# A decode kernel for attention plus gated FFN: TensorE's loop in nine guarded rounds, FFN down projection first, last loads in another order

## The chip, the cores and the metric

One core of one Trainium2 chip runs the kernel. The metric is the device time of one execution in microseconds (us). Executions of one kernel mostly agree within 0.1%. E1 to E7 and E12 below ran on one chip, E8 to E11 on another; the ratios compare each with the kernel before on its own chip.

## The reference, cut to what matters

```
x: 448 values;  16 query heads, 8 key/value heads, 65536 cached positions, head size 256, bf16
g = sigmoid(sum(x * gate_w))
a = attention(x @ wq, k_cache, v_cache) @ wo          # k_cache, v_cache: 268 MB each
b = (relu(x @ W_gate) * (x @ W_up)) @ W_down
out = g * a + (1 - g) * b                             # 448 values
```

Each cached key and value is used once, so 549 MB must come in from memory for very little arithmetic.

## The kernel before

K and V come in tiles of 8.39 MB (128 partitions x 64 KB) into three ring buffers, four K and four V tiles per key/value head, 32 of each (numbered 0 to 31 below). SyncE issues all loads in a fixed order on one queue; a load waits until the tile that had its buffer has been used. VectorE transposes a K tile in eight pieces, TensorE computes scores (64 matmuls), ScalarE exponentiates, TensorE multiplies with V tiles (64 matmuls each).

Which buffer a load takes, and so which earlier tile it waits for, is decided here:

```python
NW = H - 3
for i in range(NT - NTH + 1, NT - 1):
    order.append(("v", i, TILE))                  # V tiles 29, 30
order.append(("wo", 0, 7.3))                      # first part of wo
PIECES = [(0, 64), (64, 96), (96, 112), (112, 120), (120, 128)]
for i, (lo, hi) in enumerate(PIECES):             # V tile 31 in five pieces
    order.append(("vp", i, TILE * (hi - lo) / U))
...
ROUND = (0, 1, 2, 0, 1, 0, 2, 1)
    sl = r if m < 0 else ROUND[m % 8] if m < 8 * (H - 1) else m % 8 % 3
```

At the end this gives: K tile 31 buffer 0, V 28 buffer 1, V 29 buffer 2 (K tile 30's), V 30 buffer 0 (K tile 31's), wo buffer 1, V 31 buffer 2.

TensorE's program is straight code up to the last K tile of head 0, then a loop of seven rounds over a head each, then straight code. Inside the loop TensorE waits for a semaphore `go` that GpSimd raises once per operation (the relay), so that one loop body serves rounds that wait for different values:

```python
def emit_loop(self, its, eng, go):
    with eng.Fori(0, len(its)):
        for o in its[0]:
            eng.wait_ge(go, 1).then_inc(go, -1)
            o.fn(eng).then_inc(self.esem["pe"], 1)
```

The FFN down projection frees buffer 2 for K tile 2, and stands behind all scores of K tile 0: `max(tg + 12.2, tL["wd", 0])` sorts it there.

Of the kernel before, what the change touches and what calls it, by code (L numbers as in the profile page):

```python
# [7 lines left out]
F32 = mybir.dt.float32  # L8
# [16 lines left out]
class _Plan:  # L25
# [8 lines left out]
    def op(self, eng, key, fn, deps=()):  # L34
        o = _Op(eng, key, fn, deps)
        self.ops.append(o)
        return o

    def dma(self, eng, key, sem, fn, deps=()):
        if sem not in self.dsem:  # L40
            self.dsem[sem] = self.es.enter_context(self.nc.semaphore("d_" + sem))
        o = _Op(eng, key, fn, deps, dma=sem)
        self.ops.append(o)
        return o
# [25 lines left out]
                    o.count = ndma[o.dma]  # L70
        return progs

    def relay(self, progs, loops):

        for its in loops:
            for it in its:
                assert [o.fn.__code__ for o in it] == [o.fn.__code__ for o in its[0]]
                for o in it:
                    assert any(d.eng != "pe" for d in o.deps)
                    g = _Op("gp", o.key, None, o.deps)  # L80
                    progs["gp"].append(g)

    def emit_loop(self, its, eng, go):
        with eng.Fori(0, len(its)):
            for o in its[0]:
                eng.wait_ge(go, 1).then_inc(go, -1)  # L86
                o.fn(eng).then_inc(self.esem["pe"], 1)

    def emit(self, e, prog, eng, go=None, seen=None):
        seen = {} if seen is None else seen  # L90
# [19 lines left out]
def bass_gated_mix__gqa_block_cached__glu_gated_reglu__decode_kernel(  # L110
# [13 lines left out]
    H = A_k_cache.shape[1]  # L124
    S = A_k_cache.shape[2]
    DH = A_k_cache.shape[3]
    D = A_x.shape[2]
    F = B_W_gate.shape[1]
    NQ = A_wq.shape[1]
    J = 2 * H  # L130
    U = 128
    TK = 128 * U
    NTH = S // TK
    NT = H * NTH
    R3 = D // 128
# [10 lines left out]
    with es:  # L146
        sb = lambda name, shape, dt: es.enter_context(nc.sbuf_tensor(name, shape, dt))
        ps = lambda name, shape, dt: es.enter_context(nc.psum_tensor(name, shape, dt))

        ring = [sb("ring%d" % i, [128, U * DH], BF) for i in range(NRING)]  # L150
        P_sb = sb("P_sb", [128, 2048], BF)
        ptp = sb("ptp", [128, 1024], BF)
        scr = sb("scr", [128, 1024], BF)
# [20 lines left out]
        hT = sb("hT", [128, FT], BF)  # L174
# [2 lines left out]

        xw = P_sb[:, 0:NX * 160]
        iot = P_sb[:, 800:1056].bitcast(I32)
        qn = P_sb[:, 1056:1312]  # L180
        x_row = P_sb[0:1, 1312:1312 + D]
        fin_o = P_sb[0:1, 0:D]
        gw_row = scr[0:1, 0:D]
        xeo = scr[0:1, 448:704]
        qrep = scr[:, 704:960]
        gtmp = ptp[0:1, 0:2 * D].bitcast(F32)

        wq3 = ring[2][:, 0:R3 * NQ]
        wqh = ring[2][:, R3 * NQ:R3 * NQ + NQ // 2]
# [9 lines left out]
        OP = ps("O", [128, 512], F32)  # L199
        A_ps = ps("A_ps", [128, 512], F32)  # L200
        M_ps = ps("M_ps", [128, 512], F32)
        QN_ps = M_ps[:, 0:256]
        VT_ps = M_ps[0:2, 0:128]
        NMR_ps = M_ps[:, 128:129]
        GU_ps = M_ps[:, 448:476]
# [5 lines left out]
        pl = _Plan(nc, es)  # L211
        op, dma = pl.op, pl.dma
# [8 lines left out]
        TILE = 19.35  # L221
        order = [("wq", 0, 8.7), ("k", 0, TILE), ("gu", 0, 7.7), ("wd", 0, 3.8)]
# [2 lines left out]
            if n >= NTH - 1:  # L225
                order.append(("v", n - (NTH - 1), TILE))
        NW = H - 3
        for i in range(NT - NTH + 1, NT - 1):
            order.append(("v", i, TILE))
        order.append(("wo", 0, 7.3))  # L230
        PIECES = [(0, 64), (64, 96), (96, 112), (112, 120), (120, 128)]
        for i, (lo, hi) in enumerate(PIECES):
            order.append(("vp", i, TILE * (hi - lo) / U))

        WO = [(0, 2 * NW), (2 * NW, J - 4), (J - 4, J - 2), (J - 2, J - 1), (J - 1, J)]
        for i in range(1, 5):
# [2 lines left out]
        tL, issue = {}, []  # L239
# [4 lines left out]
        T_END = t + 20.0  # L244


        ROUND = (0, 1, 2, 0, 1, 0, 2, 1)
        slot, held, freed = {}, {2: ["gu", "dn"]}, {}
        r = 0
        for kind, i, _ in order:  # L250
            if kind in ("k", "v") or (kind, i) in (("wo", 0), ("vp", 0)):
                m = r - 3
                sl = r if m < 0 else ROUND[m % 8] if m < 8 * (H - 1) else m % 8 % 3
                slot[kind, i], freed[kind, i] = sl, held.get(sl, [])
                held[sl] = [(kind, i)]
                r += 1
# [19 lines left out]
        c_ps = []  # L276
# [45 lines left out]
        xw3 = xw.rearrange("p (kt c) -> p kt c", kt=NX)  # L322
# [1 line left out]
            xw3[:, :, 31:160:32], xT[:].unsqueeze(2).to_broadcast([128, NX, 5])[:, :, 0:5]), [x2_, c_xw])  # L324

        def f_q(e):
            for j in range(J):
                half, jj = divmod(j, J // 2)
                for kt in range(R3 + 1):
                    k_, rhs = (kt, wq3[:, kt * NQ + j * 256:kt * NQ + (j + 1) * 256]) if kt < R3 else \  # L330
                        (R3 + half, wqh[:, jj * 256:(jj + 1) * 256])
                    ins = e.matmul(QN_ps, xw3[:, k_, 31 - j:159 - j], rhs,  # L332
                                   start=(j == 0 and kt == 0), stop=(j == J - 1 and kt == R3))
            return ins



        xv = xm[:, 8:8 + H * 128].rearrange("p (h c r q a) -> p h c r q a", h=H, c=4, r=2, q=4, a=4)
        qv = qrep.rearrange("p (c h q r) -> p h c q r", c=4, q=2, r=2)

        def f_xm(e):
            for a in range(4):
# [15 lines left out]
        def f_trans(sl, w):  # L358
            v = ring[sl][:, w * 4096:(w + 1) * 4096].bitcast(U32)
            return lambda e: e.transpose(v, v)  # L360

        def f_qk(n, b, sl):
            bank = ST[n % 2]

            def f(e):
                for c in range(4):
                    for r_ in range(2):
                        x0 = 8 + (c * 2 + r_) * 16 - 8 * b
                        for w in range(4):
                            u0 = b * 64 + w * 16  # L370
                            ins = e.matmul(bank[32 * w:32 * w + 16, :], xc[:, x0:x0 + 16], ktv[sl][:, u0:u0 + 16, c, :, r_],  # L371
                                           start=(b == 0 and c == 0 and r_ == 0), stop=(b == 1 and c == 3 and r_ == 1),
                                           tile_position=(0, 32 * w))
                return ins
            return f
# [10 lines left out]
        l_, qk, smax, aexp, pv, last = {}, {}, {}, {}, {}, {}  # L386
# [41 lines left out]
        for kind, i, t in issue:  # L428
# [10 lines left out]
            elif kind == "gu":  # L439
# [18 lines left out]
                tg = tL["gu", 0]  # L458
# [4 lines left out]
            elif kind == "wd":  # L463
                a3 = dma("sp", t, "wd", lambda e: e.dma_start(wd_sb, B_W_down.rearrange("(p ft) d -> p ft d", ft=FT)), [l_["q"]])

                def f_dn(e):
                    for ft in range(FT):
                        ins = proj(e, hT[:, ft:ft + 1], wd_sb[:, ft, :], ft == 0, False)
                    return ins
                l_["dn"] = op("pe", max(tg + 12.2, tL["wd", 0]), f_dn, [l_["hT"], a3])  # L470
            elif kind == "k":
                n = i
                h, t_ = divmod(n, NTH)
                sl = slot["k", n]
                kd = dma("sp", t, "r%d" % sl, lambda e, n=n, sl=sl: e.dma_start(ring[sl][:], k_src(n)), free(("k", n)))
                tk = tL["k", n]
                tr = [op("dv", tk + 2.22 * w, f_trans(sl, w), [kd]) for w in range(8)]
                if t_ == 0:
                    xcopy = op("ac", tk + 1, lambda e, h=h: e.copy(xc[:, 8:136], xm[:, 8 + h * 128:136 + h * 128]),
                               [l_["xm"], qk.get((n - 1, 1)), c_xc])  # L480
                for b in range(2):
                    qk[n, b] = op("pe", tk + 9 * (b + 1), f_qk(n, b, sl), [tr[4 * b + 3], xcopy, aexp.get(n - 2), c_ps[n % 2]])
                NM, RS = nmb[h % 2], rs[h % 2]
                smax[n] = op("dv", tk + 22, lambda e, n=n, NM=NM, t_=t_: e.tensor_reduce(NM[:, t_:t_ + 1], ST[n % 2][:], AX.X, ALU.max, negate=True),  # L484
                             [qk[n, 1], last.get(("f", h - 2)), g_idf])
# [3 lines left out]
                if t_ == NTH - 1:  # L489
# [12 lines left out]
                    for rd in range(2):  # L502
# [10 lines left out]
                        p = op("pe", tt + 0.5, f_ptr, [rsc, g_idb, last.get(("bank", rd))])  # L513
# [7 lines left out]
                        q = op("ac", tt + 1, f_ev, [p, pv.get(h * NTH - 1)])  # L521
# [16 lines left out]
            elif kind in ("v", "vp"):  # L538
                if kind == "v":
                    n, lo, hi = i, 0, U  # L540
                    sl = slot["v", n]
                    dep = dma("sp", t, "r%d" % sl, lambda e, sl=sl, n=n: e.dma_start(ring[sl][:], v_src(n)), free(("v", n)))
                else:
                    n, (lo, hi) = NT - 1, PIECES[i]
                    sl = slot["vp", 0]
                    dep = dma("sp", t, "vp%d" % i, lambda e, sl=sl, n=n, lo=lo, hi=hi: e.dma_start(  # L546
                        ring[sl][:, lo * 256:hi * 256], v_src(n)[:, lo * 256:hi * 256]), free(("vp", 0)))
                args = (n, lo, hi, sl, tL[kind, i], dep)
                if ("tev", n // NTH) in last:
                    make_pv(*args)  # L550
                else:
                    pending.append(args)
            elif kind == "wo":
                lo, hi = WO[i]
                l_["wo", i] = dma("sp", t, "wo%d" % i, lambda e, lo=lo, hi=hi: e.dma_start(
                    wo_sb[:, lo:hi, :, :], A_wo[lo * 256:hi * 256, :].rearrange("(j p s) n -> p j s n", p=128, s=2)), free(("wo", 0)))
# [21 lines left out]
        pl.serialize(touch_m)  # L578
        progs = pl.finish()
        pe = progs["pe"]  # L580
        cut = [pe.index(qk[h * NTH + NTH - 1, 0]) for h in range(H)]
        its = [pe[a:b] for a, b in zip(cut, cut[1:])]
        go = es.enter_context(nc.semaphore("go"))
        pl.relay(progs, [its])

        pl.emit("ac", progs["ac"], nc.scalar)
        pl.emit("sp", progs["sp"], nc.sync)
        nc.sync.wait_ge(pl.dsem["out"], 16)
        pl.emit("dv", progs["dv"], nc.vector)
        pl.emit("gp", progs["gp"], nc.gpsimd, go)  # L590
        pl.emit("pe", pe[:cut[0]], nc.tensor)
        pl.emit_loop(its, nc.tensor, go)
        pl.emit("pe", pe[cut[-1]:], nc.tensor)

    return nc

# [27 lines left out]
```

## Time and profile before

Median 1280.27 us (1278.99 to 1280.39, 4 runs).

| what | value | where |
|---|---|---|
| memory traffic | 549 MB at 430 GB/s | page |
| share of 16 DMA engines, data queue | 99.6% | page |
| TensorE, VectorE busy | 33%, 50% | page |
| one K or V tile | every 19.35 us, 433.5 GB/s | timeline |
| first data packet | 1.7 us after the start | packet records |
| last pieces land | 1272.7 (first engine) to 1276.8 us (last) | landing records |

The page of the kernel before: TensorE's row, the DMA share in tenths and the GB/s over 40 slices of the span, and two DMA queues (packets, MB, share). q8 is taken as the queue that fetches TensorE's instructions: 11 packets here.

```profile
PE 427.7 (33%) x4600; PEld 169.4 (13%) x4600; DVE 633.1 (50%) x421; ACT 63.1 (5%) x124; POOL 4.1 (0%) x21
DMA  9999999999999999999999999999999999999998
GB/s 396 427 427 437 439 429 433 429 445 428 428 433 439 433 433 430 433 441 430 433 433 433 437 433 430 433 435 437 433 433 430 441 433 428 433 435 435 433 413 346
q1 hardware_dynamic: 12930, 549.03, 99.6%
q8 instruction: 11, 0.18, 0.1%
```

Read it so: the DMA engines bound the kernel (the data queue takes 99.6% of their span), and the only lost time lies in the first two slices of 32 us and the last two; in between the tiles keep coming at 433.5 GB/s.

Timeline of the kernel before around the loads of K tiles 1 and 2 (start us, duration us, engine, line, operation, in brackets the idle time before and what ended it; L382 is the down projection, L475 issues K loads, L360 transposes a K tile just landed):

```profile
59.16 1.51 PE L382 MATMUL A_ps<-ring,hT 128*1 128x224 bf16 x28
60.70 0.80 SPq L475 DMA_DIRECT2D ring<-in_A_k_cache_dram  x2
64.04 2.31 DVE L360 STREAM_TRANSPOSE ring<-ring 128x2048 uint32<-128x2048 uint32 x1 [3.96 <-DMA ring<-in_A_k_cache_dram]
84.86 4.50 DVE L360 STREAM_TRANSPOSE ring<-ring 128x2048 uint32<-128x2048 uint32 x2 [3.16 <-DMA ring<-in_A_k_cache_dram]
```

K tile 2 lands 20.82 us after K tile 1, not 19.35: its load was issued at 60.7 us, just when the queue ran out (328 GB/s from 60 to 63 us).

Timeline of the tail of the kernel before (L542 issues V tiles; L371 is the second half of a K tile's scores):

```profile
1174.49 0.80 SPq L542 DMA_DIRECT2D ring<-in_A_v_cache_dram  x2
1187.97 17.66 DVE L360 STREAM_TRANSPOSE ring<-ring 128x2048 uint32<-128x2048 uint32 x8 [12.15 <-DMA ring<-in_A_k_cache_dram]
1205.69 3.38 PE L371 MATMUL ST<-ring,xc 128*16 128x512 bf16 x32 [5.18 <-DVE ring L360]
1209.12 0.33 SPq L542 DMA_DIRECT2D ring<-in_A_v_cache_dram  x1
```

V tiles 28 and 29 are issued together at 1174.5 us. Only V tile 30 waits for the scores of K tile 31 (1209.1), and by then V tile 29 is still coming in. The windows view over these microseconds (columns: window, its length, busy us of PE, PEld, DVE, ACT and POOL with instruction counts, TensorE's granted clock, DMA share, GB/s; the share of so short a window can pass 1):

```profile
1203.00:1206.00 3.00, 0.31 (x4) 0.11 (x8) 2.64 (x2) 0.00 (x0) 0.00 (x0) 0.50 1.01 437
1206.00:1209.00 3.00, 3.00 (x32) 0.87 (x24) 0.00 (x0) 0.00 (x0) 0.00 (x0) 0.55 1.06 459
1209.00:1212.00 3.00, 0.72 (x7) 0.37 (x3) 1.45 (x5) 1.85 (x4) 0.00 (x0) 1.00 1.01 437
```

### The profile page before, as it was taken

The numbers are of one execution on the slowest core, as the hardware profiler recorded it, in microseconds if no ns is written. First come the engines' busy times: TensorE is split into PE (matmuls) and PEld (weight loads), VectorE is DVE, ScalarE is ACT, GpSimd is POOL, SyncE is SP. The second block draws the span as 40 slices with busy tenths as digits, with TensorE's granted clock in tenths as the row PEclk, the third lists the DMA queues.
The fourth block names the chain that finished last, engine by engine and source line by source line (L and its number), as shares of the span: only waits on it lengthen the run. The fifth ranks groups of instructions, "written<-read, shape, count | busy, mean of one in ns | idle before, by whom it ended". The sixth has DMA issues, their size and how long they took to land. (4 is left out here: it accounts for less than half of the span.)

```text
span 1278.8 us, 10158 instructions
## 1 busy us (share of the span) xinstructions
PE 427.7 (33%) x4600; PEld 169.4 (13%) x4600; DVE 633.1 (50%) x421; ACT 63.1 (5%) x124; POOL 4.1 (0%) x21
## 2 busy tenths in 40 slices
PE   3624323334223431224331343321433323233245
PEld 2401101111001110002110111110111101011111
DVE  2588633465433655434555444555434656335600
ACT  0000000000000100001000010000100001000000
POOL 1000000000000000000000000000000000000000
PEclk8555666656666565666656666656666656666567
DMA  9999999999999999999999999999999999999998
GB/s 396 427 427 437 439 429 433 429 445 428 428 433 439 433 433 430 433 441 430 433 433 433 437 433 430 433 435 437 433 433 430 441 433 428 433 435 435 433 413 346
DMA packets 12951, 549.27 MB, mean 430 GB/s; under 512 B 1283, under 2 KB 3590, under 8 KB 3974
## 3 DMA queue, kind: packets, MB, share of 16 engines
q1 hardware_dynamic: 12930, 549.03, 99.6%
q8 instruction: 11, 0.18, 0.1%
q14 instruction: 6, 0.05, 0.0%
q10 hardware_dynamic: 4, 0.00, 0.0%
HBM read 549.03 MB, written 0.00 MB: 429 GB/s over the span
## 5 line engine op out<-in xcount | busy, mean ns | idle before, releaser
L360 DVE STREAM_TRANSPOSE ring<-ring 128x2048 uint32<-128x2048 uint32 x256 | 565.4, 2275 | 399.0 <-DMA ring<-in_A_k_cache_dram 399.0
L371 PE MATMUL ST<-ring,xc 128*16 128x512 bf16 x2048 | 224.9, 614 | 745.8 <-PEq L86 687.6
L371 PEld LDWEIGHTS ST<-ring,xc 128*16 128x16 bf16 x2048 | 66.7, 121 | 889.6 <-issue 827.2
L402 PE MATMUL O<-ring,ptp 128*4 128x512 bf16 x2048 | 150.4, 457 | 34.1 <-DMA ring<-in_A_v_cache_dram 29.8
L486 ACT ACTIVATE P_sb<-ST,nmb 128x512 bf16<-128x512 f32 x32 | 45.1, 1411 | 1103.2 <-DVE nmb L484 1103.2
L484 DVE TENSOR_REDUCE nmb<-ST 128x1 f32<-128x512 f32 x32 | 22.1, 690 | 115.7 <-PE ST L371 115.7
L402 PEld LDWEIGHTS O<-ring,ptp 128*4 128x4 bf16 x2048 | 56.4, 99 | 127.9 <-issue 60.0
L412 DVE CAST o_sb<-O 128x512 bf16<-128x512 f32 x8 | 5.5, 692 | 80.3 <-PE O L402 80.3
L505 DVE TENSOR_TENSOR P_sb<-P_sb,hs 128x1024 bf16<-128x1024 bf16 x16 | 18.9, 1222 | 9.3 <-ACT hs L499 9.3
L510 PE MATMUL PT<-identb,P_sb 128*128 128x128 bf16 x128 | 16.2, 307 | 16.7 <-PEq L86 13.9
L452 PE MATMUL M_ps<-xT,ring 128*128 128x1 bf16 x84 | 9.5, 205 | 16.8 <-DMA ring<-in_B_W_up_dram 16.8
L510 PEld LDWEIGHTS PT<-identb,P_sb 128*128 128x128 bf16 x128 | 12.4, 139 | 19.1 <-issue 16.8
L519 ACT COPY ptp<-PT 128x256 bf16<-128x256 bf16 x32 | 10.3, 375 | 23.8 <-PE PT L510 23.8
L332 PE MATMUL M_ps<-ring,P_sb 128*128 128x256 bf16 x64 | 9.7, 329 | 2.9 <-DMA ring<-in_A_wq_dram 2.9
L452 PEld LDWEIGHTS M_ps<-xT,ring 128*128 128x128 bf16 x84 | 7.2, 152 | 17.4 <-issue 17.0
L486 ACT ACTIVATION_READ_ACCUMULATOR P_sb<-ST,nmb 128x1 f32 x32 | 8.4, 263 | 0.0
L332 PEld LDWEIGHTS M_ps<-ring,P_sb 128*128 128x128 bf16 x64 | 7.5, 119 | 4.9 <-issue 3.0
L455 PE MATMUL M_ps<-xT,ring 128*64 128x1 bf16 x56 | 7.8, 276 | 0.0
L435 DVE STREAM_TRANSPOSE scr<-P_sb 128x128 uint32<-128x128 uint32 x1 | 0.3, 313 | 12.8 <-ACT P_sb L434 12.8
L495 PE MATMUL M_ps<-identf,hs 128*2 128x128 f32 x8 | 2.5, 308 | 10.9 <-PEq L86 9.7
L382 PE MATMUL A_ps<-ring,attnT 128*1 128x224 bf16 x64 | 4.6, 305 | 2.7 <-DMA ring<-in_A_wo_dram 2.7
L455 PEld LDWEIGHTS M_ps<-xT,ring 128*64 128x64 bf16 x56 | 5.4, 191 | 0.4
(74 smaller groups left out, 61.5 us busy)
## 6 DMA issues: line engine op xcount, KB each, us to landing
ring<-in_A_v_cache_dram SPq DMA_DIRECT2D x1, 4096.0 KB, 30.0
ring<-in_A_wq_dram SPq DMA_DIRECT2D x1, 3072.0 KB, 10.2
ring<-in_A_wo_dram SPq DMA_DIRECT2D x1, 2240.0 KB, 32.4
ring<-in_A_v_cache_dram SPq DMA_DIRECT2D x1, 2048.0 KB, 24.6
ring<-in_B_W_down_dram SPq DMA_DIRECT2D x1, 1568.0 KB, 21.2
ring<-in_B_W_gate_dram SPq DMA_DIRECT2D x1, 1344.0 KB, 32.8
ring<-in_B_W_up_dram SPq DMA_DIRECT2D x1, 1344.0 KB, 35.5
ring<-in_A_v_cache_dram SPq DMA_DIRECT2D x1, 1024.0 KB, 26.6
```

The source lines that it names most:

```text
L332: ins = e.matmul(QN_ps, xw3[:, k_, 31 - j:159 - j], rhs, start=(j == 0 and kt == 0), stop=(j == J - 1 and kt == R3))
L360: return lambda e: e.transpose(v, v)
L371: ins = e.matmul(bank[32 * w:32 * w + 16, :], xc[:, x0:x0 + 16], ktv[sl][:, u0:u0 + 16, c, :, r_], start=(b == 0 and c == 0 and r_ == 0), ...
L402: ins = e.matmul(OP[32 * g:32 * g + 4, :], ptp[:, col:col + 13:4], ring[sl][:, k * 512:(k + 1) * 512], start=(a == 0 and k < 4), stop=(a = ...
L412: o1 = op("dv", tn, lambda e: e.tensor_copy(o_sb[:], OP[:]), [pv[n], last.get(("otr", h - 1))])
L452: e.matmul(GU_ps[:, c:c + 1], wf3[which][:, kt * F + ft:(kt + 1) * F:FT], xT[:, kt:kt + 1], start=(kt == 0), stop=False, skip_group_check= ...
L455: ins = e.matmul(GU_ps[64 * half:64 * half + 64, c:c + 1], wfh[which][:, ft:F // 2:FT], xT[:, R3 + half:R3 + half + 1], start=False, stop= ...
L484: smax[n] = op("dv", tk + 22, lambda e, n=n, NM=NM, t_=t_: e.tensor_reduce(NM[:, t_:t_ + 1], ST[n % 2][:], AX.X, ALU.max, negate=True), [q ...
L486: aexp[n] = op("ac", tk + 23, lambda e, n=n, t_=t_, NM=NM, RS=RS: e.activation(P_sb[:, t_:2048:4], ST[n % 2][:], ACTF.Exp, bias=NM[:, t_:t ...
L505: rsc = op("dv", tt, lambda e, X=X, pb=pb: e.tensor_tensor(pb, pb, X[:, 12:16].unsqueeze(1).to_broadcast([128, 256, 4]), ALU.mult), [h7, a ...
L510: ins = e.transpose(PT[rd][:, s * 128:(s + 1) * 128], P_sb[:, (rd * 8 + s) * 128:(rd * 8 + s + 1) * 128], identb[:, :])
L519: ins = e.copy(dst, src)
```

## The change

Its evident intent: put nearly all of TensorE's program into the loop, so that less code is fetched; issue K tile 2 earlier; halve the number of q matmuls. For one loop body to serve all heads, a part must use the same buffers in every round, so V tile 29 moves to the buffer that V tiles 1, 5, 9... use, which is K tile 31's, and the order of the last loads is adapted. At the end the changed kernel has K tile 31 in buffer 0, V 28 in 1, V 29 in 0 (K tile 31's), V 31 in 2, V 30 in 0 (V 29's), wo in 1.

```diff
-    def emit_loop(self, its, eng, go):
-        with eng.Fori(0, len(its)):
-            for o in its[0]:
-                eng.wait_ge(go, 1).then_inc(go, -1)
+    def emit_loop(self, n, parts, eng, go):
+        with eng.Fori(0, n) as i:
+            ...
+            for lo, hi, rounds in parts:
+                with ExitStack() as st:
+                    if lo > 0:
+                        st.enter_context(eng.If_ne(i, lo - 1))
+                    if hi < n:
+                        st.enter_context(eng.If_lt(i, hi))
+                    body(rounds[0])
...                                   # q: 32 matmuls of 512 columns, a PSUM bank of its own
-            for j in range(J):
+            for h in range(H):
...                                   # the last loads
-        for i in range(NT - NTH + 1, NT - 1):
-            order.append(("v", i, TILE))
-        order.append(("wo", 0, 7.3))
-        for i, (lo, hi) in enumerate(PIECES):
-            order.append(("vp", i, TILE * (hi - lo) / U))
+        pieces = [("vp", i, TILE * (hi - lo) / U) for i, (lo, hi) in enumerate(PIECES)]
+        order += [("v", NT - 3, TILE), pieces[0], ("v", NT - 2, TILE), ("wo", 0, 7.3)] + pieces[1:]
+        LASTS = (0, 1, 0, 2, 0, 1)
-    ... else m % 8 % 3
+    ... else LASTS[m - 8 * (H - 1)]
...                                   # down projection before all scores of K tile 0
-                l_["dn"] = op("pe", max(tg + 12.2, tL["wd", 0]), f_dn, [l_["hT"], a3])
+                l_["dn"] = op("pe", tg + 12.2, f_dn, [l_["hT"], a3])
-                    qk[n, b] = op("pe", tk + 9 * (b + 1), f_qk(n, b, sl), ...)
+                    qk[n, b] = op("pe", tk + (9 * (b + 1) if n else 20 + b), f_qk(n, b, sl), ...)
...                                   # only K tile 0 and V tile 31 outside the loop of H + 1 rounds
+        span = [(1, H + 1), (1, H), (1, H + 1), (0, H), (1, H + 1), (0, H), (1, H)]
+        pl.emit("pe", pe[:heads[0][0]], nc.tensor)
+        pl.emit_loop(H + 1, span, nc.tensor, go)
+        pl.emit("pe", pe[end:], nc.tensor)
```

More of the change, by code (lines that the diff above doesn't have):

```diff
@@ L71, in finish, with relay, body @@
         return progs
-    def relay(self, progs, loops):
-        for its in loops:
-            for it in its:
-                assert [o.fn.__code__ for o in it] == [o.fn.__code__ for o in its[0]]
-                for o in it:
-                    assert any(d.eng != "pe" for d in o.deps)
-                    g = _Op("gp", o.key, None, o.deps)
-                    progs["gp"].append(g)
-    def emit_loop(self, its, eng, go):
-        with eng.Fori(0, len(its)):
-            for o in its[0]:
-                eng.wait_ge(go, 1).then_inc(go, -1)
-                o.fn(eng).then_inc(self.esem["pe"], 1)
+    def relay(self, progs, prog):
+        for o in prog:
+            assert any(d.eng != "pe" for d in o.deps)
+            progs["gp"].append(_Op("gp", o.key, None, o.deps))
+    def emit_loop(self, n, parts, eng, go):
+        with eng.Fori(0, n) as i:
+            i = i.val.handles[0]
+            def body(ops):
+                for o in ops:
+                    eng.wait_ge(go, 1).then_inc(go, -1)
+                    o.fn(eng).then_inc(self.esem["pe"], 1)
+            for lo, hi, rounds in parts:
+                assert all([o.fn.__code__ for o in r] == [o.fn.__code__ for o in rounds[0]] for r in rounds)
+                assert len(rounds) == hi - lo
+                with ExitStack() as st:
[4 more added lines that the diff above has]
+                    body(rounds[0])
     def emit(self, e, prog, eng, go=None, seen=None):
@@ L179, in bass_gated_mix__gqa_block_cached__glu_gated_reglu__decode_kernel @@
         iot = P_sb[:, 800:1056].bitcast(I32)
-        qn = P_sb[:, 1056:1312]
-        x_row = P_sb[0:1, 1312:1312 + D]
+        qn = P_sb[:, 1056:1568]
+        x_row = P_sb[0:1, 2048 - D:2048]
         fin_o = P_sb[0:1, 0:D]
@@ L184, in bass_gated_mix__gqa_block_cached__glu_gated_reglu__decode_kernel @@
         xeo = scr[0:1, 448:704]
-        qrep = scr[:, 704:960]
+        qrep = scr[:, 512:1024]
         gtmp = ptp[0:1, 0:2 * D].bitcast(F32)
@@ L201, in bass_gated_mix__gqa_block_cached__glu_gated_reglu__decode_kernel @@
         M_ps = ps("M_ps", [128, 512], F32)
-        QN_ps = M_ps[:, 0:256]
+        QN_ps = ps("QN", [128, 512], F32)[:]
         VT_ps = M_ps[0:2, 0:128]
@@ L252, in bass_gated_mix__gqa_block_cached__glu_gated_reglu__decode_kernel @@
                 m = r - 3
-                sl = r if m < 0 else ROUND[m % 8] if m < 8 * (H - 1) else m % 8 % 3
+                sl = r if m < 0 else ROUND[m % 8] if m < 8 * (H - 1) else LASTS[m - 8 * (H - 1)]
                 slot[kind, i], freed[kind, i] = sl, held.get(sl, [])
@@ L326, in f_q @@
         def f_q(e):
-            for j in range(J):
-                half, jj = divmod(j, J // 2)
+            for h in range(H):
+                half, hh = divmod(h, H // 2)
                 for kt in range(R3 + 1):
-                    k_, rhs = (kt, wq3[:, kt * NQ + j * 256:kt * NQ + (j + 1) * 256]) if kt < R3 else \
-                        (R3 + half, wqh[:, jj * 256:(jj + 1) * 256])
-                    ins = e.matmul(QN_ps, xw3[:, k_, 31 - j:159 - j], rhs,
-                                   start=(j == 0 and kt == 0), stop=(j == J - 1 and kt == R3))
+                    k_, rhs = (kt, wq3[:, kt * NQ + h * 512:kt * NQ + (h + 1) * 512]) if kt < R3 else \
+                        (R3 + half, wqh[:, hh * 512:(hh + 1) * 512])
+                    ins = e.matmul(QN_ps, xw3[:, k_, 31 - h:159 - h], rhs,
+                                   start=(h == 0 and kt == 0), stop=(h == H - 1 and kt == R3))
             return ins
         xv = xm[:, 8:8 + H * 128].rearrange("p (h c r q a) -> p h c r q a", h=H, c=4, r=2, q=4, a=4)
-        qv = qrep.rearrange("p (c h q r) -> p h c q r", c=4, q=2, r=2)
+        qv = qrep.rearrange("p (q c h r) -> p h c q r", q=2, c=4, r=2)
         def f_xm(e):
@@ L469, in f_dn @@
                     return ins
-                l_["dn"] = op("pe", max(tg + 12.2, tL["wd", 0]), f_dn, [l_["hT"], a3])
+                l_["dn"] = op("pe", tg + 12.2, f_dn, [l_["hT"], a3])
+                assert tg + 12.2 < tL["k", 0] + 20
             elif kind == "k":
@@ L481, in bass_gated_mix__gqa_block_cached__glu_gated_reglu__decode_kernel @@
                 for b in range(2):
-                    qk[n, b] = op("pe", tk + 9 * (b + 1), f_qk(n, b, sl), [tr[4 * b + 3], xcopy, aexp.get(n - 2), c_ps[n % 2]])
+                    qk[n, b] = op("pe", tk + (9 * (b + 1) if n else 20 + b), f_qk(n, b, sl), [tr[4 * b + 3], xcopy, aexp.get(n - 2), c_ps[n % 2]])
                 NM, RS = nmb[h % 2], rs[h % 2]
@@ L547, in bass_gated_mix__gqa_block_cached__glu_gated_reglu__decode_kernel @@
                         ring[sl][:, lo * 256:hi * 256], v_src(n)[:, lo * 256:hi * 256]), free(("vp", 0)))
-                args = (n, lo, hi, sl, tL[kind, i], dep)
+                args = (n, lo, hi, sl, tL[kind, i] if (kind, i) != ("vp", 0) else tL["v", NT - 2] + 0.1, dep)
                 if ("tev", n // NTH) in last:
@@ L580, in bass_gated_mix__gqa_block_cached__glu_gated_reglu__decode_kernel @@
         pe = progs["pe"]
-        cut = [pe.index(qk[h * NTH + NTH - 1, 0]) for h in range(H)]
-        its = [pe[a:b] for a, b in zip(cut, cut[1:])]
         go = es.enter_context(nc.semaphore("go"))
-        pl.relay(progs, [its])
+        heads = []
+        for n in range(1, NT):
+            heads.append((pe.index(qk[n, 0]), max((n - NTH + 1) % NTH * 2 - 1, 0), n))
+        for n in range(1, NT - 1):
+            if n % NTH:
+                heads.append((pe.index(pv[n]), n % NTH * 2, n))
+        heads = sorted(heads)
+        end = pe.index(pv[NT - 2]) + 1
+        parts = [[] for _ in range(7)]
+        for (a, p, n), (b, _, _) in zip(heads, heads[1:] + [(end, 0, 0)]):
+            parts[p].append(pe[a:b])
+        span = [(1, H + 1), (1, H), (1, H + 1), (0, H), (1, H + 1), (0, H), (1, H)]
+        span = [(lo, hi, p) for (lo, hi), p in zip(span, parts)]
+        pl.relay(progs, pe[heads[0][0]:end])
         pl.emit("ac", progs["ac"], nc.scalar)
@@ L590, in bass_gated_mix__gqa_block_cached__glu_gated_reglu__decode_kernel @@
         pl.emit("gp", progs["gp"], nc.gpsimd, go)
-        pl.emit("pe", pe[:cut[0]], nc.tensor)
-        pl.emit_loop(its, nc.tensor, go)
-        pl.emit("pe", pe[cut[-1]:], nc.tensor)
+        pl.emit("pe", pe[:heads[0][0]], nc.tensor)
+        pl.emit_loop(H + 1, span, nc.tensor, go)
+        pl.emit("pe", pe[end:], nc.tensor)
     return nc
```

## The prediction

> **What bounds the kernel now.** The DMA engines. The page moves 549.03 MB at 430 GB/s, its one large queue busy 99.6% of 16 engines' span. In the timeline K and V tiles (8.39 MB) land every 19.35 us: 433.5 GB/s. [...] TensorE is busy 33%, VectorE 50%. Only moments when a DMA engine has nothing queued, and the spread among the 16, can be won: 2.1 us before the first packet, about 1 us at 61 us, and the tail, where the last pieces land on the first engine 4.1 us before the last (packet and landing records). Some 5 us, 0.4%, are at stake.
>
> **What the change does.**
> 1. *Start.* K tile 2's load waits for the down projection, now behind K tile 0's scores: issued at 60.7 us (timeline), while the queue runs dry at 61.2 to 61.9; K tile 2 lands 20.8 us after K tile 1. After, the projection follows gate/up (end 52.8) and takes 1.5 us: issue near 55.3. Gain 1.0 to 1.4 us.
> 2. *Code.* TensorE's program shrinks from about 2800 to 1950 instructions. The instruction queue moves 11 packets of 16 KB, one per some 256 instructions[...]; each held its DMA engine 1.0 us and slowed the next packet by 0.5 us. Some 7 or 8 remain. Only the last engine matters: 0 to 1.5 us. The loop (about 1100 instructions in both) was not fetched again per round and should not be now. Branches are off the critical path.
> 3. *q by 512 columns.* 64 matmuls take 9.7 us; perhaps 2 us less, off the path.
> 4. *Tail.* The loop fixes each part's ring buffer, so V tile 29 now takes K tile 31's buffer (before: K tile 30's). Its load waits for K tile 31's last score: 17.7 us of transposes plus 3.4 us of scores after that tile lands, while V tile 28, the only load queued, ends after 19.35 us. With 0.5 us from packet to semaphore and 1.3 to 1.7 us from issue to first packet, the slowest engine idles about 3.5 us, the fastest over 6; a restart made first packets some 0.7 us slower. Afterwards all engines start level, so part of the 4.1 us spread goes; 68 us of loads follow. V tile 31's first half, in a free buffer, covers V tile 29's matmuls (6.5 us against 9.7 us of load): no second gap.
>
> **Sum.** Before, the last landing is at 1276.8. After, K tile 31 lands 1.3 us earlier; V tile 29's first packet comes at 1209.3, plus 0.7; 68.5 us later the ordinary engine is done (1278.5), one with a code fetch in the tail at about 1280. That is 1.7 to 3.2 us later: about 1282.6 us, range 1280.0 to 1285.2. Chances: faster by over 2% 0.005, within 0.975, slower 0.02.
>
> **What would show it.** K tile 2's issue near 55 us, landing 19.4 us after K tile 1; under 10 fetch packets of 16 KB; in the DMA queue's own waits, V tile 29's issue waiting for TensorE's scores until about 1208 us; the DMA share over 1203 to 1211 us well below 1, once; a smaller landing spread at the end; still 2 us from last landing to the end.
>
> **What would make it wrong.** If the jumps over parts, or the longer loop, make TensorE fetch code again every round (five blocks, nine rounds, about 1.5 us each over 16 engines: 4 us more), it is slower. If the level start removes more spread than I think, or fetches hit no late engine, it is equal or up to 1 us faster.

Read from the kernel before: a 16 KB packet took 1.02 us (median of 11) and the data packet behind it 0.49 us longer; landings came 0.5 us after an engine's last packet; the first packets came 1.0 to 1.7 us after the first issue began, the first of all at 1.7 us in the timeline's clock (the prediction has 2.1); the first packets after the gap at 61 us took 3.15 us against 2.42. The 2 us for q rest on no run. The 4 us for fetching again are an estimate from the packets: 1100 instructions in five of them, nine rounds, 1.5 us each over 16 engines.

## The result, and the profile after

The changed kernel takes 1283.43 us (median of 4 runs, 1283.25 to 1283.85) against 1280.27. Ratio 1.0027, 95% interval 1.001 to 1.0045: slower by a quarter of a per cent. A ratio is the mean time of one kernel's runs over that of the other's of the same rounds, so it is not quite the ratio of the medians.

The page of the changed kernel, the lines that answer to those above:

```profile
PE 421.9 (33%) x4568; PEld 166.7 (13%) x4568; DVE 633.4 (49%) x421; ACT 63.3 (5%) x124; POOL 4.1 (0%) x21
DMA  9999999999999999999999999999999999999898
GB/s 399 446 427 432 431 440 429 434 431 440 429 434 431 436 431 434 434 436 431 434 434 436 431 434 434 436 431 434 431 438 429 436 431 438 429 436 431 360 423 346
q1 hardware_dynamic: 12930, 549.03, 99.3%
q8 instruction: 7, 0.11, 0.0%
```

The second slice has risen from 427 to 446 GB/s, seven code fetches remain of eleven, and a new hole stands in the third slice from the end (360 GB/s, from 1186 to 1218 us). The start, in the timeline of the changed kernel (L388 is the down projection, L482 issues K loads):

```profile
53.51 2.40 PE L388 MATMUL A_ps<-ring,hT 128*1 128x224 bf16 x24 [0.54 <-DVE hT L467]
56.32 0.33 SPq L482 DMA_DIRECT2D ring<-in_A_k_cache_dram  x1
63.48 4.50 DVE L366 STREAM_TRANSPOSE ring<-ring 128x2048 uint32<-128x2048 uint32 x2 [2.36 <-DMA ring<-in_A_k_cache_dram]
82.82 4.51 DVE L366 STREAM_TRANSPOSE ring<-ring 128x2048 uint32<-128x2048 uint32 x2 [1.68 <-DMA ring<-in_A_k_cache_dram]
```

K tile 2 is issued 4.4 us earlier and lands 19.34 us after K tile 1. The tail, in the timeline of the changed kernel:

```profile
1173.31 0.33 SPq L549 DMA_DIRECT2D ring<-in_A_v_cache_dram  x1
1186.75 17.66 DVE L366 STREAM_TRANSPOSE ring<-ring 128x2048 uint32<-128x2048 uint32 x8 [12.10 <-DMA ring<-in_A_k_cache_dram]
1204.61 3.37 PE L377 MATMUL ST<-ring,xc 128*16 128x512 bf16 x32 [5.16 <-PEq L86]
1208.02 0.33 SPq L549 DMA_DIRECT2D ring<-in_A_v_cache_dram  x1
1208.39 0.43 SPq L553 DMA_DIRECT2D ring<-in_A_v_cache_dram  x1
1236.11 0.33 SPq L549 DMA_DIRECT2D ring<-in_A_v_cache_dram  x1
```

K tile 31 still lands 1.22 us earlier than before (1186.75 against 1187.97). But now V tile 28 goes out alone at 1173.3, and V tile 29 at 1208.02, when the scores of K tile 31 end (in the DMA queue's own waits from 1170 us on, 34.4 us of waiting for line L377, the scores). The windows view shows what the DMA engines did meanwhile:

```profile
1203.00:1206.00 3.00, 1.39 (x16) 0.59 (x20) 1.41 (x1) 0.00 (x0) 0.00 (x0) 0.50 0.05 22
1206.00:1209.00 3.00, 1.98 (x24) 0.45 (x12) 0.90 (x3) 0.24 (x1) 0.00 (x0) 0.74 0.19 66
1209.00:1212.00 3.00, 0.62 (x3) 0.37 (x3) 1.40 (x3) 1.61 (x4) 0.00 (x0) 0.83 0.90 328
```

The trace also records when each of the 16 engines reported the end of each load. First, middle and last engine, in us (these records, and the times of code fetches below, lie about 0.2 us after the timeline's clock; the columns "E1" and "E3" are two experiments below):

```
               before                    changed                   E1                        E3
K tile 31      1185.4 1186.8 1188.2      1184.1 1185.2 1187.0      1184.2 1185.1 1187.2      1185.4 1186.6 1190.2
V tile 28      1204.7 1206.2 1207.5      1203.5 1204.6 1206.3      1203.5 1204.4 1206.6      1204.7 1206.0 1209.6
V tile 29      1224.1 1225.8 1226.9      1229.5 1229.7 1230.2      1222.9 1223.8 1225.9      1232.9 1232.9 1234.6
last load      1272.7 1274.3 1276.8      1278.4 1278.8 1280.0      1271.4 1273.0 1274.3      1281.6 1282.0 1283.7
```

From V tile 28 to V tile 29 the last engine takes 23.9 us instead of 19.35, a loss of 4.5; the first takes 26.0. The spread between the engines, 2.8 us before the gap, is 0.7 after it, since all start again within 0.8 us (first packets at 1209.0 to 1209.75 us in the timeline's clock); before the change it stays and reaches 4.1 at the end. Only the last engine counts, and it ends 3.1 us later than before, the middle one 4.5. Part of that difference is a fetch in the kernel before: its last engine, level with the next until 1246.2, is 1.5 us behind it when wo's first part lands (1253.8 against 1252.3), just after a code fetch of 16 KB at 1251.3 us, and ends last.

### The profile page after: what moved, and what is told of

It is laid out like the page before. It is cut to its first block, busy times and chain, and to the rows that moved or that the text cites. A ratio compares the mean times of both kernels' runs of the same rounds, so it can differ in the third digit from the quotient of the medians.

```text
span 1282.0 us, 10210 instructions
## 1 busy us (share of the span) xinstructions
PE 421.9 (33%) x4568; PEld 166.7 (13%) x4568; DVE 633.4 (49%) x421; ACT 63.3 (5%) x124; POOL 4.1 (0%) x21
## 5 line engine op out<-in xcount | busy, mean ns | idle before, releaser
L377 PE MATMUL ST<-ring,xc 128*16 128x512 bf16 x2048 | 223.3, 609 | 748.3 <-PEq L86 748.3
L377 PEld LDWEIGHTS ST<-ring,xc 128*16 128x16 bf16 x2048 | 67.9, 120 | 890.4 <-issue 889.4
L408 PE MATMUL O<-ring,ptp 128*4 128x512 bf16 x2048 | 146.3, 448 | 41.0 <-PEq L86 37.0
L526 ACT COPY ptp<-PT 128x256 bf16<-128x256 bf16 x32 | 10.3, 375 | 23.9 <-PE PT L517 23.9
L340 PE MATMUL QN<-ring,P_sb 128*128 128x512 bf16 x32 | 9.0, 452 | 2.8 <-DMA ring<-in_A_wq_dram 2.8
L458 PEld LDWEIGHTS M_ps<-xT,ring 128*128 128x128 bf16 x84 | 7.2, 152 | 17.7 <-issue 17.3
L388 PE MATMUL A_ps<-ring,attnT 128*1 128x224 bf16 x64 | 4.6, 305 | 0.6 <-DMA ring<-in_A_wo_dram 0.6
```

The costliest lines, as they stand in the source:

```text
L340: ins = e.matmul(QN_ps, xw3[:, k_, 31 - h:159 - h], rhs, start=(h == 0 and kt == 0), stop=(h == H - 1 and kt == R3))
L377: ins = e.matmul(bank[32 * w:32 * w + 16, :], xc[:, x0:x0 + 16], ktv[sl][:, u0:u0 + 16, c, :, r_], start=(b == 0 and c == 0 and r_ == 0), ...
L408: ins = e.matmul(OP[32 * g:32 * g + 4, :], ptp[:, col:col + 13:4], ring[sl][:, k * 512:(k + 1) * 512], start=(a == 0 and k < 4), stop=(a = ...
L458: e.matmul(GU_ps[:, c:c + 1], wf3[which][:, kt * F + ft:(kt + 1) * F:FT], xT[:, kt:kt + 1], start=(kt == 0), stop=False, skip_group_check= ...
L526: ins = e.copy(dst, src)
```

## The experiments

Theory: V tile 29's wait for K tile 31's scores drains the DMA queue and costs 4 to 5 us; the early down projection gives back 1.2; everything else is near zero. Rival: the guarded loop (branches, relay, code fetches) costs the time. A second question is what the code fetches do at all.

### E1, E2, E3, E4: the parts of the change by themselves

E1 keeps the changed kernel's start and its nine guarded rounds, and takes the tail of the kernel before:

```diff
-        order += [("v", NT - 3, TILE), pieces[0], ("v", NT - 2, TILE), ("wo", 0, 7.3)] + pieces[1:]
+        ... the order of the kernel before; its buffers (m % 8 % 3) too
-        span = [(1, H + 1), (1, H), (1, H + 1), (0, H), (1, H + 1), (0, H), (1, H)]
+        span = [(1, H + 1), (1, H), (1, H), (0, H), (1, H), (0, H), (1, H)]   # V tiles 29, 30 out of the loop
-        end = pe.index(pv[NT - 2]) + 1
+        end = pe.index(pv[NT - 4]) + 1
```

> The changed kernel (early down projection, wide q, nine guarded rounds) with the tail of the kernel before: V tile 29 in K tile 30's buffer, V tiles 29 and 30 out of the loop, pieces last. Theory (V tile 29's load waits for K tile 31's scores and 16 DMA engines run dry): the dip to 10 lanes near 1204 to 1209 us is gone, V tiles 28 and 29 land 19.4 us apart instead of 23.9, and the start's 1.2 us stay won: 1277.7 to 1279.2 us, faster than both kernels. Rival (the guarded loop, its branches and code fetches cost the time): it stays near 1283.

E2 is the kernel before with only these two lines:

```diff
-                l_["dn"] = op("pe", max(tg + 12.2, tL["wd", 0]), f_dn, [l_["hT"], a3])
+                l_["dn"] = op("pe", tg + 12.2, f_dn, [l_["hT"], a3])
-                    qk[n, b] = op("pe", tk + 9 * (b + 1), ...
+                    qk[n, b] = op("pe", tk + (9 * (b + 1) if n else 20 + b), ...
```

> The kernel before with only the down projection ahead of K tile 0's scores. Theory: K tile 2's load is issued near 56 us instead of 60.7, K tile 2 lands 19.4 us after K tile 1 instead of 20.8, and nothing later gives it back: 1.0 to 1.4 us less, 1278.8 to 1279.3 us. Rival (the early gain comes from the smaller program): no change, 1280.2.

E3 is the kernel before, its loop of seven rounds kept, with only the changed order and buffers of the tail:

```diff
+        order += [("v", NT - 3, TILE), pieces[0], ("v", NT - 2, TILE), ("wo", 0, 7.3)] + pieces[1:]
+        LASTS = (0, 1, 0, 2, 0, 1)
-    ... else m % 8 % 3
+    ... else LASTS[m - 8 * (H - 1)]
```

> The kernel before, its loop of seven rounds and its start, with only the load order and the buffers of the changed tail. Theory: the same gap as in the changed kernel without any guard: V tile 29's issue waits for the scores of K tile 31, V tiles 28 and 29 land 23.9 us apart, 1283.5 to 1285.3 us. Rival (guarded loop): about 1280.

E4 is the kernel before with only the q matmuls of 512 columns (`for h in range(H)`, their PSUM bank and the wider copies).

> The kernel before with only q by 512 columns, in a PSUM bank of its own. Both theories: nothing, since q is done 10 us before K tile 0 lands: within 0.5 us of 1280.2.

| run | median us (5 runs, range) | ratio to before, 95% interval |
|---|---|---|
| E1, old tail | 1277.71 (1277.45 to 1278.12) | 0.9987, 0.9973 to 1.0001 |
| E2, start only | 1278.31 (1277.94 to 1278.55) | 0.9991, 0.9978 to 1.0005 |
| E3, tail only | 1285.33 (1284.05 to 1286.95) | 1.0044, 1.003 to 1.0058 |
| E4, q only | 1279.53 (1278.93 to 1280.44) | 1.0001, 0.9987 to 1.0014 |

The kernel before ran 9 times beside them: 1279.47 us (1278.00 to 1281.07). The windows view of E1, and then of E3, over the gap:

```profile
1203.00:1206.00 3.00, 1.14 (x12) 0.44 (x16) 1.67 (x1) 0.00 (x0) 0.00 (x0) 0.58 1.06 459
1206.00:1209.00 3.00, 2.46 (x24) 0.60 (x16) 0.50 (x1) 0.00 (x0) 0.00 (x0) 0.50 0.96 415
1209.00:1212.00 3.00, 0.93 (x3) 0.58 (x3) 1.01 (x5) 1.85 (x4) 0.00 (x0) 0.50 1.01 437
```

```profile
1203.00:1206.00 3.00, 0.00 (x0) 0.00 (x0) 3.00 (x3) 0.00 (x0) 0.00 (x0) 0.50 0.31 131
1206.00:1209.00 3.00, 1.30 (x16) 0.43 (x20) 1.65 (x1) 0.00 (x0) 0.00 (x0) 0.50 0.05 22
1209.00:1212.00 3.00, 2.26 (x24) 0.51 (x16) 0.68 (x1) 0.00 (x0) 0.00 (x0) 0.65 0.00 0
```

In E2's trace K tile 2 is issued at 56.26 us and lands 19.35 us after K tile 1, as expected. (E2's median lies 0.5 us under its range, E4's 0.2 us under, E3's at the upper edge; the kernel before too was 0.8 us faster in this set.)

E1, with all the guards, is 5.7 us under the changed kernel (by the last landing, and by the medians of two sets; 5.1 by the ratios) and has no gap (the "10 lanes" of its expectation stand in no view here; the gap's DMA share in the changed kernel was 0.05 and 0.19). E3, without any guard, has the same gap and is the slowest. The rival falls: the tail's load order is the loss. E2's gain agrees with the 1.22 us by which K tile 31 lands earlier in the changed kernel, though its interval still touches 1. E4 shows no change, as expected: q is finished long before it is needed. The group lines of q before and in the changed kernel show how small the gain was even locally (busy us, mean ns of one, then idle before and its cause):

```profile
L332 PE MATMUL M_ps<-ring,P_sb 128*128 128x256 bf16 x64 | 9.7, 329 | 2.9 <-DMA ring<-in_A_wq_dram 2.9
```

```profile
L340 PE MATMUL QN<-ring,P_sb 128*128 128x512 bf16 x32 | 9.0, 452 | 2.8 <-DMA ring<-in_A_wq_dram 2.8
```

E1 is the fastest kernel, with every run below the median of the kernel before, but its gain over that is small: 0.13% by ratio, with an interval that just touches 1. What E1 has beyond E2 (smaller program, wide q) is worth 0.04% by ratio, which these runs can't tell from nothing.

E3 is 5.6 us slower than before by ratio, more than the gap's 4.5 us. In its trace the last engine is already 2 us later at K tile 31 (1190.2 against 1188.2) while the middle one is not. The landings show when: its distance to the next engine jumps from 0.4 to 1.45 us at 442 to 445 us and to 2.4 us at 872 us, where 8 KB packets of another instruction queue (q14) fall, both times on the engine that is already last. In the kernel before, such packets at the same two places leave the last engines level (0.04 us or less). Its five runs also scatter over 2.9 us; that the place of such packets changes from run to run would explain it, but only one of the five was profiled, so this is not shown.

### E7: filling the gap from the queue

E7 is the changed kernel with V tile 31's first piece queued ahead of V tile 29, and the first part of wo ahead of V tile 30. (One more edited line, left out here, keeps the matmuls of wo after V tile 30's, where they were.)

```diff
-        order += [("v", NT - 3, TILE), pieces[0], ("v", NT - 2, TILE), ("wo", 0, 7.3)] + pieces[1:]
+        order += [pieces[0], ("v", NT - 3, TILE), ("wo", 0, 7.3), ("v", NT - 2, TILE)] + pieces[1:]
-        LASTS = (0, 1, 0, 2, 0, 1)
+        LASTS = (0, 1, 2, 0, 1, 0)
```

> The changed kernel with the first piece of V tile 31 queued ahead of V tile 29, and the first output weights ahead of V tile 30. Theory (what costs is only what is queued while V tile 29 waits): 9.7 us of load now cover the 4 to 6 us gap at 1204 us, which vanishes; V tile 30 still waits for V tile 29's matmuls, about 7.8 us, and 5.3 us of weights cover that, so a smaller gap of 2 to 3.5 us appears there: 1280.3 to 1282. Rival (guarded loop): unchanged at 1283.4.

Measured: 1281.27 us (1280.88 to 1282.16), ratio 1.0017 (1.0003 to 1.003). The windows view of E7, at the old place of the gap and at the new one:

```profile
1203.00:1206.00 3.00, 1.29 (x16) 0.50 (x20) 1.51 (x1) 0.00 (x0) 0.00 (x0) 0.50 0.94 404
1206.00:1209.00 3.00, 2.30 (x24) 0.54 (x16) 0.66 (x1) 0.00 (x0) 0.00 (x0) 0.63 0.91 393
1239.00:1242.00 3.00, 1.75 (x35) 0.55 (x24) 0.00 (x0) 0.00 (x0) 0.00 (x0) 1.00 0.69 233
1242.00:1245.00 3.00, 0.00 (x0) 0.00 (x0) 0.00 (x0) 0.00 (x0) 0.00 (x0) 1.00 0.66 262
```

The first gap is gone without a change to the loop; what was queued did it. A smaller one comes at V tile 30, which now has only 5.3 us of weights before it: on the last engine it lands 27.5 us after V tile 29 (1235.5 to 1263.0), where 19.35 us for the tile and 5.8 for the weights, as they landed here, would make 25.2. The loss is thus 2.3 us instead of 4.5.

### E5, E8 to E12: the second gap and the code fetch in the tail

The changed kernel's trace also showed a second gap, which the prediction had excluded: at 1239 to 1240.7 us two of the 16 engines idled 1.3 and 1.7 us, because V tile 30's load, issued at 1236.1, did not reach them in time. E5 makes the piece that covers this wait longer:

```diff
-        PIECES = [(0, 64), (64, 96), (96, 112), (112, 120), (120, 128)]
+        PIECES = [(0, 80), (80, 96), (96, 112), (112, 120), (120, 128)]
```

> The changed kernel with V tile 31's first piece 80 of 128 key groups instead of 64, so that 12.1 us of load instead of 9.7 us stand between V tile 29's landing and the need for V tile 30's load. Theory (the prediction's 'no second gap' was wrong: two of 16 DMA engines idle 1.3 and 1.7 us at 1239 to 1241 us, and these are the last ones at the end): that idle time is gone and the last landing comes about 1.2 us earlier: 1281.8 to 1282.8 us. Rival (the two engines are late for another reason, such as code fetches): unchanged, 1283.4.

Measured: 1283.48 us (1283.38 to 1283.59), ratio 1.0031. The expectation failed. The gap is gone (V tile 30's landings spread over 0.8 us instead of 1.9), and the time is the same. In E5's trace a code fetch of 16 KB at 1271.9 us falls on one engine, which from then on is 0.8 us behind the next and ends last. E8 and E9 should move that fetch out of the tail, by 70 extra one-column matmuls near 5 us, when TensorE has nothing to do (they repeat the same product, so the result stays):

```diff
-            for kt in range(NX):
+            for kt in list(range(NX)) * 15:      # E8 (on E5) and E9 (on the changed kernel); * 9 in E12 (on E5)
```

> The changed kernel with V tile 31's first piece of 80 key groups (no second gap) and 70 idle repeats of a one-column matmul near 5 us, before TensorE has anything else to do, which move the last code fetch that lies in the tail (at 1272 us in the run of the 80-group piece) by about 140 instructions, to before the tail or to its very end. Theory (removing the second gap gained nothing because that fetch, 1.5 us on one DMA engine, then ended last): with both gone no engine stands out in the tail, the spread of the last landings falls from 1.6 to about 1 us: 1282.3 to 1283.0 us, 0.5 to 1 us less than the changed kernel. Rival (the end is set by something else, such as the issue of the last loads): 1283.4, as both others.

> The changed kernel with only the 70 idle matmuls, so the fetch leaves the tail but the second gap (two engines, 1.3 and 1.7 us) stays. Theory: those two engines end last as before, no change: 1283.2 to 1283.6. Rival (only the fetch mattered): as little as the run with both, about 1282.6.

> The changed kernel again, unchanged, on the same chip as the others of this set: 1283.4 us, ratio 1.0027 to the kernel before. Last landings spread by about 1.6 us, two engines late from the second gap.

> The 80-group piece again on the same chip: within 0.3 us of the changed kernel, one engine late by the fetch in the tail, no second gap.

> The 80-group piece with 40 idle matmuls instead of 70. With 70 the code fetch only went from 1272 to 1274 us and still put one engine 1.0 us behind the next; counting back, 40 should put it after the last load, near 1280 us. Theory: no code fetch of 16 KB between 1230 us and the last load's landing, the last landing 0.3 us or less behind the next to last, 1279.1 to 1279.4 us, and 1282.4 to 1283.1 us in all. Rival (the fetch does not set the end): 1283.6.

| run | median us (5 runs, range) | ratio | 16 KB fetch in the tail, us | last landing, next to last, us |
|---|---|---|---|---|
| E10, changed kernel again | 1283.69 (1283.38 to 1284.02) | 1.0033 | 1269.8 | 1280.1, 1279.5 |
| E9, 70 idle matmuls | 1283.91 (1283.77 to 1284.14) | 1.0034 | 1275.7 | 1280.8, 1280.5 |
| E11, E5 again | 1283.65 (1283.04 to 1283.99) | 1.0031 | 1271.7 | 1280.7, 1279.8 |
| E8, E5 with 70 | 1283.65 (1283.30 to 1284.07) | 1.0033 | 1274.2 | 1280.1, 1279.1 |
| E12, E5 with 40 | 1282.95 (1282.77 to 1283.03) | 1.0027 | 1279.5 | 1279.5, 1279.3 |

E8 and E9 missed their purpose: the fetch moved by 2 to 6 us and stayed in the tail, so they tell nothing against either theory. They were run on another chip. E12 placed it at 1279.5 us, after the last load's data. Then, and only then, no engine stands out (landings of the last load spread over 0.65 us), and the time falls by 0.5 to 0.7 us, every run below every run of E5, E8, E9, E10 and E11. So a single code fetch of 16 KB in the last 10 us costs this kernel 0.5 to 0.7 us here (E5 ran on E12's chip; the ratios, 1.0031 and 1.0027, have overlapping intervals, so the claim rests on the times and the landings together). E10 also showed that the second gap comes and goes: in that trace of the unchanged program all 16 engines had their load in time, at the same total time. It was not worth what E5's expectation gave it: in the changed kernel's trace the engine of the second gap and that of the fetch, followed from landing to landing, end within 0.01 us of each other, so taking away the gap alone could gain nothing. No run has the gap without a fetch in the tail, so what the gap costs alone is not shown.

### E6: what code fetches cost

E6 is the kernel before with TensorE's program unrolled, without loop and relay:

```diff
-        pl.relay(progs, [its])
-        pl.emit("pe", pe[:cut[0]], nc.tensor)
-        pl.emit_loop(its, nc.tensor, go)
-        pl.emit("pe", pe[cut[-1]:], nc.tensor)
+        pl.emit("pe", pe, nc.tensor)
```

> The kernel before with TensorE's program fully unrolled, no loop and no relay: about 36 fetch packets of 16 KB instead of 11. Theory (a fetch costs one DMA engine 1.5 us, and the engine with most fetches ends last): 25 more fetches over 16 engines, 2.4 us each on average, so 1282 to 1284.5 us. Rival (fetches are free under other queues' work): 1280.2; and if the loop itself cost time (branches, relay), it would be under 1280.

Measured: 1284.34 us (1284.05 to 1285.31), ratio 1.0039 (1.0026 to 1.0053). The instruction queue on E6's page:

```profile
q8 instruction: 36, 0.59, 0.2%
```

Each 16 KB packet took 1.07 us (median of 36), and the 64 KB data packet right behind it took 0.49 us longer than the usual 2.42. The amounts by which it is longer repeat with period eight through the whole trace (0.545, 0.546, 0.490, 0.494, 0.503, 0.464, 0.464, 0.477 us, and again), so the fetches seem to go round eight of the 16 engines; the trace does not name the engine, so this is an inference. The first nine fetches of the kernel before give the same values in the same order (0.477, 0.547, 0.545, 0.490, 0.493, 0.503, 0.465, 0.463, 0.477). By these numbers (36 fetches, 1.07 + 0.49 us each) one engine would have four or five fetches of 1.5 us and another none, which is an estimate. The landings agree: by V tile 28 their spread in E6 is 7.7 us (2.8 before), and the last landing is 4.6 us later than before, the middle one 3.3. The expected mean of 2.4 us over 16 engines was in the right direction; the last engine had more.

## Why the prediction was right, point by point

- **Start: right.** K tile 2's issue was foretold near 55.3 and came at 56.3; it landed 19.34 us after K tile 1; K tile 31 landed 1.22 us earlier (1.3 foretold). E2's trace shows the earlier issue and landing by themselves; its gain in time, 0.09%, is not clear of noise.
- **Code: right in count, open in gain.** Seven fetches of 16 KB ("some 7 or 8"), none between 107.3 and 1270.9 us, so the rounds of the guarded loop in that time were not fetched again; the loop before had none between 244.6 and 1180.3 us. "Some 256 instructions" to a packet fits E6's page: 9200 matmuls and weight loads, 36 packets. The branches' cost does not show: E1, with all guards, took 1277.71 us, E2 without any 1278.31. "0 to 1.5 us" for fewer fetches could not be measured apart; E6 shows the sign, and E12 the size of one fetch in the last 10 us (0.5 to 0.7 us).
- **q: the local gain was mis-sized, without effect.** 0.6 us (9.67 to 9.04) instead of 2, since the matmuls ran 452 ns each against 329; off the path, as E4 shows.
- **Tail: right.** Issue at 1208.02 ("about 1208"), DMA share 0.05 and 0.19 where it had been 1, idle times of 3.4 to 7.0 us on the engines ("about 3.5, the fastest over 6"; the last packets ended at 1202.7 to 1205.6 us in the timeline's clock), first packets 0.6 to 1.4 us after the end of the issuing instruction (1208.35 us) and some 0.6 us slower (median 3.01 us against 2.42). E1 and E3 show that this, and not the loop, is the loss.
- **"No second gap": wrong.** The step compared TensorE's 6.5 us with 9.7 us of load and left out that a load can take longer to reach all engines: issued at 1236.11 us, V tile 30's reached two of them only 4.0 and 4.3 us later. In one trace two engines idled 1.3 and 1.7 us; in another none did. What it alone costs in time is not shown.
- **Sum: 0.8 us low.** Last landing foretold at 1278.5 for an ordinary engine and "about 1280" for one with a code fetch in the tail; measured 1278.8 (middle) and 1280.0 (last). The profiled span ends at 1282.0, and the median of the timed runs is 1.4 us longer, which makes 1283.4. The prediction's 1282.6 lay between the two engines instead of at the last one. Thus what was mis-sized was which engine to take: the kernel ends with the last one. That the fetch fell in the tail at all was foreseen only as a possibility, and the range was 5.2 us wide; E1, E3 and E7 test the mechanism better than the sum does.

## What to carry to other kernels

When transfers bound a kernel, ask of every moved load which earlier work must end before it may be issued, and how many microseconds of transfers are queued behind which it can hide; here one tile of 19.35 us could not hide 17.7 + 3.4 us of work plus the restart. A loop that fixes buffers per part can force such a wait, so take the few tiles at the end out of the loop (E1: 5.7 us) rather than bend the order of loads to it. And follow the slowest of the DMA engines, not their mean: a thing as small as a 16 KB code fetch put one engine 0.8 us behind the next (E5), and a late one stayed late here while the queue was full (in the kernel before the spread was 2.8 us at 85 us and still 2.8 at 1188).
